# Third chunk's loads in parts, and one piece moved in the order of a mixture-of-experts kernel

## The chip, the cores and the metric

The kernel runs on one core of one Trainium2 chip. The metric is the device time of one execution in microseconds; lower is better. The core's engines are TensorE (PE; its weight loads are listed apart as PEld), VectorE (DVE), ScalarE (ACT), GpSimd (POOL) and SyncE (SP), which issues most of the DMAs. Each engine works through its own instructions in the order in which the program gives them, and waits for others by semaphores.

## The reference

Attention over q, k and v of shape (4, 8, 576, 64) makes x of shape (2304, 512); a mixture of eight experts over x makes the output.

```python
# attention, for each batch and head
q_d, k_d, v_d = means of q, k, v over 4 neighbouring tokens      # 144 of them
out_d = softmax(scale * q_d k_d^T) v_d, repeated 4 times
scores = scale * q k^T, kept where |i - j| < 4                   # a window of 7 tokens
x = out_d + softmax(scores) v                                    # (2304, 512)
# experts
P = exp(x w_gate - max); 8 times: P /= rows' sums; P /= columns' sums; P *= N / E
out = sum over e of P[:, e] * (relu(x w1[e]) w2[e])              # w1 512x1024, w2 1024x512
```

## The kernel before, in words

**Chunks and units of attention.** The 576 groups of four tokens (144 for each batch) are cut into six chunks: three small ones of 64 groups (256 tokens) and three of 128 groups (512 tokens). The third chunk (`c` = 2) covers groups 128 to 191 and so lies on both sides of a batch's end at 144. A small chunk is one load unit for all heads, a large one two, so there are nine units `u` (`lunits`); the third chunk is `u` = 2. For each unit three tiles are loaded: a window of k, q, and a window of v (`l_load_win`, `l_load_q`). `l_parts` says into how many parts such a load falls: eight for the third chunk (four groups of heads by two batches), four for the second chunk and for the two units each of the fourth and fifth, two for those of the last. A k or v part of the third chunk is two DMAs, a q part one.

**The windowed attention** (`l_gen`) is VectorE's: for each unit four products with k (L1162) and their sums (L1188), a softmax, and four products with v (L1238) and their sums (L1311). The down-sampled attention (`d_gen`) is made of small matmuls on PE, with ScalarE between them; its inputs are sums over the loaded tiles that GpSimd makes (`p_gen`, L1415 and L1419) and that go through memory. `x_gen` joins both into the chunk's x, split into a high part xh and a low part xl.

**The experts.** The list `order` holds pairs of a piece and an expert. A piece is one chunk or the first two together; a small chunk alone has two tiles of 128 tokens, (0, 1) and a large chunk have four. Each pair is eight steps, one for each 128 of the 1024 hidden columns; such a step is called a unit of the experts here, and they are counted from 0 along `order`. Each step loads 256 KB of w1 (L1004) and 256 KB of w2 (L1009), splits both into a high part on ScalarE (L2233) and a low part on GpSimd (L2256) or VectorE (L2252), and runs 12 matmuls of the first layer (L2100), the split of the hidden tile (ScalarE L2164, VectorE L2167), and three matmuls for each tile in the second (L2134 to L2136). The weights have six raw buffers, three steps ahead. A step of a two-tile piece takes half of PE's time and the same loads and splits as one of a four-tile piece.

The first three pairs are chunk 0 with experts 0, 1 and 2 (steps 0 to 23); then (0, 1) with 3, 4 and 5 (24 to 47), the third chunk with 3 (48 to 55), (0, 1) with 6, chunk 0 with 7, the third chunk with 4 (72 to 79), chunk 3 with 3 (80 to 87), the third chunk with 5 (88 to 95), and so on. A pair's result is copied out to memory (spilled) while attention is not done. When attention ends, the pairs that are finished by then (`n_done`) stay, the rest of the list is put in a new order, and later stages do most of the remaining work by a Strassen scheme with seven products in place of eight.

**What sets the order of the work.** A planner in the program (`sched`) runs when the kernel is built. It has a clock for each engine, for SyncE's issuing (`clk["sp"]`) and for the transfers (`clk["dma"]`), and generators that each offer their next step with the time at which it can start; the earliest step is emitted, a rank decides between equals. `ld_gen` is the generator for the loads of the units `u` = 2 on: when the products of the unit before have read its k tile (`k_free`) it emits the whole load of k and of q, and when they have read its v tile (`v_free`) that of v. `m_next` is the number of the expert steps whose first layer has been emitted. The function `dma(kb)` advances both clocks and returns the time at which the planner takes the data to be there. All these loads, and the weight loads, are on SyncE's one queue, in the order emitted; a weight load waits there until its raw buffer has been read.

Of the kernel before, what the change touches and what calls it, by code (L numbers as in the profile page):

```python
# [8 lines left out]
F32 = mybir.dt.float32  # L9
# [793 lines left out]
def attention_moe_kernel(  # L803
# [11 lines left out]
    B, H, S, D = q.shape  # L815
# [3 lines left out]
    R = 4  # L819
# [4 lines left out]
    NF = FF // 128  # L824
# [11 lines left out]
    def is_small(c):  # L836
        return chunks[c][1] == 64
# [50 lines left out]
    ap1 = att.enter_context(tc.tile_pool(name="ap1", bufs=1, side="right"))  # L888
# [7 lines left out]
    def mask_of(c):  # L896
        i = edged.index(c)
        return mask[:, i * 2 * R * W:(i + 1) * 2 * R * W]
# [24 lines left out]
    def segs(t0, n):  # L923
        done = 0
        while done < n:
            b, g = divmod(t0 + done, SD)
            step = min(n - done, SD - g)
            yield done, step, b, g
            done += step


    clk = {"pe": 0.0, "dve": 0.0, "act": 0.0, "pool": 0.0, "dma": 0.0, "sp": 0.0, "port": 0.0}
# [25 lines left out]
    def dma(kb, *deps):  # L958
        clk["sp"] = max([clk["sp"]] + list(deps)) + 0.35
        clk["dma"] = max(clk["dma"], clk["sp"] + 0.6) + 0.05 + kb * 0.55  # L960
        return clk["dma"] + 2.0
# [85 lines left out]


    lunits = [(c, hh) for c in range(NC) for hh in range(1 if is_small(c) else 2)]
    l_q, l_k, l_v, l_out = {}, {}, {}, {}  # L1050
    l_done = {}
    x_taken = {}
    lo_keys = []
# [1 line left out]
    def l_parts(c, hh):  # L1055
        t0, n = chunks[c]
        m = n // 2
        return [
            (m * i + off // 2, k_ // 2, b, g // 2, (0 if is_small(c) else 4 * hh) + 2 * i)
            for i in range(128 // m) for off, k_, b, g in segs(t0, n)  # L1060
        ]

    def l_load_q(u, s0=0, sn=2, eng=None):
        if u >= len(lunits):
            return
        c, hh = lunits[u]
        if s0 == 0:
            l_q[u] = (ap1.tile([128, 2, 2 * R, D], F32, tag="lq", name="lq"), [])
        t, ready = l_q[u]
        for p0, m, b, g, h0 in l_parts(c, hh):  # L1070
            (eng or nc.sync).dma_start(
                out=t[p0:p0 + m, s0:s0 + sn].rearrange("p h r d -> p h (r d)"),
                in_=q[b, h0 + s0:h0 + s0 + sn, 2 * R * g:2 * R * (g + m), :].rearrange(
                    "h (p r) d -> p h (r d)", r=2 * R
                ),
            )
        ready += [dma(2 * sn)] * sn

    def l_load_win(u, src, dst, step=2, before=None):
        if u >= len(lunits):  # L1080
            return
        c, hh = lunits[u]
        t = ap2.tile([128, 2, WR, D], F32, tag="lw", name="lw")
        if c == 0:
            nc.gpsimd.memset(t[0:1, 0:step, 0:R - 1, :], 0.0)
        if c == NC - 1:
            nc.gpsimd.memset(t[96:128, :, WR - (R - 1):WR, :], 0.0)

        def win(p0, m, b, g, h0, lo, hi):
            if u + (src is v) and hi - lo > 2 * R:  # L1090
                win(p0, m, b, g, h0, lo, lo + 2 * R)
                return win(p0, m, b, g, h0, lo + 2 * R, hi)
            row = (b * H + h0 + s0) * S + 2 * R * g - (R - 1) + lo
            nc.sync.dma_start(  # L1094
                out=t[p0:p0 + m, s0:s0 + step, lo:hi, :].rearrange("p h r d -> p h (r d)"),
                in_=bass.AP(src.tensor, row * D, [[2 * R * D, m], [S * D, step], [1, (hi - lo) * D]]),
            )

        ready = []
        for s0 in range(0, 2, step):  # L1100
            if before is not None:
                before(s0, step)
            for p0, m, b, g, h0 in l_parts(c, hh):
                if c == 0 and h0 + s0 == 0:
                    win(p0, 1, b, g, h0, R - 1, WR)
                    win(p0 + 1, 15, b, g + 1, h0, 0, WR)
                    win(p0 + 16, m - 16, b, g + 16, h0, 0, WR)
                elif c == NC - 1 and h0 + s0 + step == H and 2 * R * (g + m) == S:
                    win(p0, m - 16, b, g, h0, 0, WR)
                    win(p0 + m - 16, 15, b, g + m - 16, h0, 0, WR)  # L1110
                    win(p0 + m - 1, 1, b, g + m - 1, h0, 0, WR - (R - 1))
                else:
                    win(p0, m, b, g, h0, 0, WR)
            ready += [dma(7 * step / 2)] * step
        dst[u] = (t, ready)

    alone = [True]
# [216 lines left out]
            p2_t[r] = max(clk["act"], t_p2[r]) if r < 2 else t_p2[r]  # L1334

    def ld_gen():
        for u in range(1, len(lunits) - 1):
            while u not in k_free or u >= U1 and ((u, 1) not in s_read or (u, 0) not in s_read):
                yield None
            t = max([k_free[u]] + [s_read[u, s] for s in (0, 1) if u >= U1])  # L1340
            yield t + HOP, "sp", 0.0, False
            l_load_win(u + 1, k, l_k)
            yield t + HOP, "sp", 0.0, False
            l_load_q(u + 1)
            while u not in v_free or u >= U1 and (u, 2) not in s_read:
                yield None
            t = max([v_free[u]] + [s_read[u, 2] for _ in (0,) if u >= U1])
            yield t + HOP, "sp", 0.0, False
            l_load_win(u + 1, v, l_v)


    halves = [(b, hf) for b in range(B) for hf in range(2)]
# [714 lines left out]
    m_next = [0]  # L2067
# [316 lines left out]
    with tc.manual_schedule():  # L2384
# [10 lines left out]
        EH = 3  # L2395
        order = [
            ((0,), 0), ((0,), 1), ((0,), 2), ((0, 1), 3), ((0, 1), 4), ((0, 1), 5), ((2,), 3), ((0, 1), 6), ((0,), 7),
            ((2,), 4), ((3,), 3), ((2,), 5), ((3,), 4), ((2,), 6), ((3,), 5), ((3,), 6), ((3,), 7),
        ]
        last = [((1, 2), 7)]  # L2400
        order += [(p_, e) for e in reversed(range(EH)) for p_ in ((3,), (1, 2))]
        for c, e in order:
            for f in range(NF):
                units.append((e, f, lambda: wa))
                todo.extend(p_todo(len(units) - 1))
        l_load_win(0, k, l_k, step=1, before=lambda h_a, h_n: l_load_q(0, h_a, h_n, None if h_a else nc.scalar))
        d_load()
        l_load_win(0, v, l_v)
# [20 lines left out]
        for big in (True, False):  # L2429
# [7 lines left out]
            for c in edged:  # L2437
                if is_small(c) == big:
                    continue
                t0, n = chunks[c]  # L2440
                at_ = [pb for pb in range(0, n + 1, 2) if (t0 + pb) % SD == 0]
                assert len(at_) == 1
                z = WR * at_[0] // 2
                a, z = z - (R - 1) if at_[0] else z, z + R - 2 if at_[0] < n else z - 1
                dst = mask_of(c)
# [88 lines left out]
        th["lo"] = Thread(lo_gen())  # L2534
        th["raw"] = Thread(raw_gen())
        th["ld"] = Thread(ld_gen())
        for i in range(n_cv[0]):
            w1_done[i], w2_done[i] = w_ready[i]
# [9 lines left out]
        n = m_end[0] // NF * NF  # L2548
# [360 lines left out]
```

## Time and profile before

| | |
|---|---|
| median of 3 runs | 1576.42 us (1576.12 to 1576.99) |
| the profiled execution | 1578.05 us |
| its span, first to last instruction | 1576.3 us |
| granted clock of TensorE, mean share | 0.999 |
| PE busy | 1562.4 us, 99% of the span |
| VectorE, GpSimd, ScalarE busy | 1340.4, 1071.8, 827.1 us |
| tiles spilled (DMA issues of spill<-sp) | 40 |

Times in the trace are microseconds from the span's first instruction. A row of the timeline gives start, duration, engine, line, operation, tile written and tiles read, shape and the number of like instructions merged; in brackets stands the engine's idle time before it and what ended it. "SPq" is SyncE's queue, and its durations are those of issuing. A matmul's record lasts longer than the time after which PE can start the next, so neighbouring records overlap.

### The profile page before, as it was taken

How to read it: one execution, taken by the hardware profiler on the slowest of the kernel's cores; microseconds unless marked ns; L12 is line 12 of the kernel's file. 1: busy time of each engine (PE TensorE's matmuls, PEld its weight loads, DVE VectorE, ACT ScalarE, POOL GpSimd, SP SyncE). 2: the span in 40 equal slices, each digit the busy share in tenths (PEclk: the TensorE clock that was granted, in tenths of full speed). 3: DMA queues.
4: the chain of work that ended last, by engine and by line, in shares of the span. 5: the costliest groups of instructions: out<-in, count | busy, mean ns of one | idle time of the engine just before them, and what ended most of it. 6: DMA issues, size and time to landing. Idle time of an engine off the chain costs nothing.

```text
span 1576.3 us, 24605 instructions
## 1 busy us (share of the span) xinstructions
PE 1562.4 (99%) x8220; PEld 1321.4 (84%) x8220; DVE 1340.4 (85%) x1880; ACT 827.1 (52%) x1763; POOL 1071.8 (68%) x998
## 2 busy tenths in 40 slices
PE   9999999999999999999999999999999999999998
PEld 7788888888888888889999988888888888888887
DVE  8688998778988687478999797999999999999987
ACT  4564554555455534365555545555555555555553
POOL 5698666868685600278777548877877787877872
PEclk9999999999999999999999999999999999999999
DMA  8878676768585645513332372212221222221102
GB/s 197 209 207 209 166 182 156 217 178 231 149 218 135 185 136 174 159 52 102 99 117 73 110 218 82 74 54 67 60 72 57 74 59 75 62 68 54 48 14 54
DMA packets 230701, 191.23 MB, mean 121 GB/s; under 512 B 26478, under 2 KB 188462, under 8 KB 230574
## 3 DMA queue, kind: packets, MB, share of 16 engines
q1 hardware_dynamic: 224046, 178.39, 41.9%
q10 hardware_dynamic: 6528, 11.28, 2.0%
q8 instruction: 64, 1.05, 0.3%
q14 instruction: 63, 0.52, 0.1%
HBM read 167.42 MB, written 22.18 MB: 120 GB/s over the span
## 4 chain that ended last, share of the span: by engine, by line
PE 93%; issue 2%; DVE 2%; DMA 1%; SPq 1%; POOL 1%; ACT 1%; ACTq 0%; POOLq 0%; DVEq 0%
PE psm L588 27%; PE psm L600 19%; PE psh L2100 18%; PE psm L783 7%; PE psy L2134 6%; PE psy L2135 6%; PE psy L2136 6%; PE pss L1725 1%; PE psg L1905 1%; SPq L1094 1%; DMA r<-in_moe_w_dram 0%; PE psx L1849 0%; PE psd L1787 0%; PE psd L1758 0%; DMA dr<-in_v_dram 0%
## 5 line engine op out<-in xcount | busy, mean ns | idle before, releaser
L571 POOL TENSOR_TENSOR o<-r,o 128x512 fp32r<-128x512 f32 x126 | 165.8, 1316 | 87.9 <-ACT o L567 87.4
L2256 POOL TENSOR_TENSOR w1l<-r,w1h 128x512 fp32r<-128x512 f32 x112 | 158.4, 1414 | 81.2 <-ACT w1h L2233 74.5
L2256 POOL TENSOR_TENSOR w2l<-r,w2h 128x512 fp32r<-128x512 f32 x114 | 157.3, 1380 | 28.0 <-ACT w2h L2233 26.9
L588 PE MATMUL psm<-th,o 128*128 128x512 f32 x512 | 173.1, 389 | 0.0
L2134 PE MATMUL psy<-w2h,hh 128*128 128x512 f32 x408 | 165.4, 405 | 0.0
L622 DVE TENSOR_TENSOR acc<-psm,acc 128x512 f32<-128x512 f32 x216 | 144.6, 682 | 21.0 <-PE psm L600 20.8
L2135 PE MATMUL psy<-w2l,hh 128*128 128x512 f32 x408 | 159.5, 391 | 0.0
L2136 PE MATMUL psy<-w2h,hl 128*128 128x512 f32 x408 | 159.4, 391 | 0.0
L600 PE MATMUL psm<-hx,o 128*128 128x512 f32 x564 | 151.1, 389 | 0.0
L2164 ACT ACTIVATE hh<-psh 128x512 fp32r<-128x512 f32 (+1 forms) x136 | 67.6, 497 | 158.4 <-PE psh L2100 149.3
L571 POOL TENSOR_TENSOR o<-xh,o 128x256 fp32r<-128x256 f32 x132 | 111.2, 849 | 50.6 <-ACT o L567 38.4
L2167 DVE SCALAR_TENSOR_TENSOR hl<-psh,hh 128x512 fp32r<-128x512 f32 (+1 forms) x136 | 76.2, 560 | 73.2 <-ACT hh L2164 73.0
L2233 ACT ACTIVATE w2h<-r 128x512 fp32r<-128x512 f32 x133 | 83.7, 629 | 91.3 <-PE psy L2136 25.8
L588 PE MATMUL psm<-xh,o 128*128 128x512 f32 x384 | 131.2, 389 | 0.3 <-DVE hl L2352 0.3
L2100 PE MATMUL psh<-xhs,w1h 128*128 128x256 f32 (+1 forms) x384 | 124.7, 325 | 0.3 <-ACT xhs L1866 0.3
L600 PEld LDWEIGHTS psm<-hx,o 128*128 128x128 f32 x564 | 105.8, 188 | 22.0
L2100 PE MATMUL psh<-xhs,w1l 128*128 128x256 f32 (+1 forms) x384 | 122.5, 319 | 1.5 <-DVE w1l L2252 1.5
L2100 PE MATMUL psh<-xls,w1h 128*128 128x256 f32 (+1 forms) x384 | 122.3, 319 | 0.2
L567 ACT ACTIVATE o<-r 128x512 fp32r<-128x512 f32 x139 | 87.3, 628 | 55.4 <-PE psm L600 35.5
L588 PEld LDWEIGHTS psm<-th,o 128*128 128x128 f32 x512 | 96.1, 188 | 20.1
L1311 DVE TENSOR_REDUCE lo<-prod 128x256 f32<-128x1792 f32 x32 | 109.4, 3420 | 0.4
L571 POOL TENSOR_TENSOR xh<-xh,xh 128x256 fp32r<-128x256 f32 x32 | 24.8, 782 | 118.1 <-ACT xh L567 118.1
(346 smaller groups left out, 4574.4 us busy)
## 6 DMA issues: line engine op xcount, KB each, us to landing
r<-in_moe_w_dram SPq DMA_DIRECT2D x367, 256.0 KB
xh<-in_moe_w_dram SPq DMA_DIRECT2D x108, 128.0 KB
spill<-sp ACTq DMA_DIRECT2D x40, 256.0 KB
s<-spill SPq DMA_DIRECT2D x40, 256.0 KB
xl<-in_moe_w_dram SPq DMA_DIRECT2D x68, 128.0 KB
g<-gd SPq DMA_DIRECT2D x16, 256.0 KB
sums<-dr SPq DMA_DIRECT2D x36, 64.0 KB
r2x<-in_moe_w_dram SPq DMA_DIRECT2D x9, 256.0 KB
```

Of the source, the lines that this page charges most:

```text
L567: self.nc.scalar.activation(out=self.get(v)["h"], in_=self.w_view(l, r, ps), func=AF.Copy)
L571: (self.nc.gpsimd if pool else self.nc.vector).tensor_tensor(out=o["l"], in0=self.w_view(l, r, ps), in1=o["h"].bitcast(F32), op=ALU.subtract)
L588: self.nc.tensor.matmul(out=ps, lhsT=wt[:, k], rhs=xt[:, k], start=start and n == 0, stop=n == 5, skip_group_check=not start,)
L600: self.nc.tensor.matmul(out=ps, lhsT=wt[:, a, 128 * m:128 * m + 128], rhs=ht, start=start and n == 0, stop=n == 5, skip_group_check=not start,
L622: self.nc.vector.tensor_tensor(out=self.get(o[0]), in0=self.get(a[0]), in1=self.get(b[0]), op=op)
L783: self.nc.tensor.matmul(out=ps, lhsT=self.at_tile(ht, t), rhs=wt[:, a], start=start and n + t % 2 == 0, stop=n == 5, skip_group_check=not ...
L1311: nc.vector.tensor_reduce(out=ot[:, :, h % 2], in_=pr.rearrange("p r w d -> p r d w"), axis=AX.X, op=ALU.add,)
L2100: nc.tensor.matmul(out=ps, lhsT=w[:, kk], rhs=x[:, kk], start=(kk == 0 and j == 0), stop=(kk == 3 and j == 2),)
L2134: nc.tensor.matmul(out=ye[z], lhsT=hh[:, ts], rhs=h2, start=(f2 == 0), stop=False)
L2135: nc.tensor.matmul(out=ye[z], lhsT=hh[:, ts], rhs=l2, start=False, stop=False)
L2136: nc.tensor.matmul(out=ye[z], lhsT=hl[:, ts], rhs=h2, start=False, stop=(f2 == NF - 1))
L2256: nc.gpsimd.tensor_tensor(out=l, in0=r, in1=h.bitcast(F32), op=ALU.subtract)
```

## The change

The two load functions become generators, `l_q_parts` and `l_win_parts`, that stop after each part; the old names run them to the end at once. A q load is announced (`l_q[u]`) only when all its parts are out. The planner's clock is charged for each part by itself, with 0.4 us of SyncE more for each part of k and v. In `ld_gen` the loads go through `paced`, which for `u` = 2 alone waits after each part (for v, after the first and then after every second one) until `m_next` has moved, so that another expert step has been emitted; and k of `u` = 2 waits until eight steps have been. In `order`, the third chunk with expert 5 stands before chunk 3 with expert 3.

```diff
-    def l_load_q(u, s0=0, sn=2, eng=None):
+    def l_load_q(*a, **z):
+        for _ in l_q_parts(*a, **z):
+            pass
+
+    def l_load_win(*a, **z):
+        for _ in l_win_parts(*a, **z):
+            pass
+
+    def l_q_parts(u, s0=0, sn=2, eng=None):
...
-        for p0, m, b, g, h0 in l_parts(c, hh):
+        for n, (p0, m, b, g, h0) in enumerate(l_parts(c, hh)):
+            if n:
+                yield
+            t_in = dma(sn / 4)
             (eng or nc.sync).dma_start(
...
-        ready += [dma(2 * sn)] * sn
-
-    def l_load_win(u, src, dst, step=2, before=None):
+        ready += [t_in] * sn
+        l_q[u] = q_tile[u]
+
+    def l_win_parts(u, src, dst, step=2, before=None):
...
-            for p0, m, b, g, h0 in l_parts(c, hh):
+            for n, (p0, m, b, g, h0) in enumerate(l_parts(c, hh)):
+                if n:
+                    yield
+                clk["sp"] += 0.4
+                t_in = dma(7 * step / 16)
...
-            ready += [dma(7 * step / 2)] * step
+            ready += [t_in] * step
...
     def ld_gen():
+        n_alone = 3 * NF
+
+        def paced(u, it, of=1):
+            for i, _ in enumerate(it):
+                n = m_next[0]
+                while u == 2 and i % of == 0 and m_next[0] == n:
+                    yield None
+
         for u in range(1, len(lunits) - 1):
             while u not in k_free or u >= U1 and ((u, 1) not in s_read or (u, 0) not in s_read):
                 yield None
+            while u == 1 and m_next[0] < NF:
+                yield None
             t = max([k_free[u]] + [s_read[u, s] for s in (0, 1) if u >= U1])
             yield t + HOP, "sp", 0.0, False
-            l_load_win(u + 1, k, l_k)
+            yield from paced(u + 1, l_win_parts(u + 1, k, l_k))
             yield t + HOP, "sp", 0.0, False
-            l_load_q(u + 1)
+            yield from paced(u + 1, l_q_parts(u + 1))
             while u not in v_free or u >= U1 and (u, 2) not in s_read:
                 yield None
             t = max([v_free[u]] + [s_read[u, 2] for _ in (0,) if u >= U1])
             yield t + HOP, "sp", 0.0, False
-            l_load_win(u + 1, v, l_v)
+            yield from paced(u + 1, l_win_parts(u + 1, v, l_v), 2)
...
-            ((2,), 4), ((3,), 3), ((2,), 5), ((3,), 4), ((2,), 6), ((3,), 5), ((3,), 6), ((3,), 7),
+            ((2,), 4), ((2,), 5), ((3,), 3), ((3,), 4), ((2,), 6), ((3,), 5), ((3,), 6), ((3,), 7),
```

## Rows read from the trace of the kernel before

**Rows 1.** The page's busy times: engine, us, share of the span, instructions.

```profile
PE 1562.4 (99%) x8220; PEld 1321.4 (84%) x8220; DVE 1340.4 (85%) x1880; ACT 827.1 (52%) x1763; POOL 1071.8 (68%) x998
```

**Rows 2.** PE's waits: line, whom it waited for, us in total, times, longest.

```profile
PE psh L2100 <- DVE w1l L2252: 1.5, 2, 1.2
...
PE pss L1725 <- ACT qz L1675: 1.0, 1, 1.0
...
PE psd L1758 <- ACT pt L1763: 0.4, 1, 0.4
...
PE psx L1849 <- DVE lo L1311: 0.3, 1, 0.3
```

**Rows 3.** SyncE's queue in time, 66 to 117 us: start, us of issuing, what.

```profile
66.32 0.37 SPq L1004 DMA_DIRECT2D r<-in_moe_w_dram  x1
66.74 6.38 SPq L1094 DMA_DIRECT2D lw<-in_k_dram  x16
73.25 0.36 SPq L1009 DMA_DIRECT2D r<-in_moe_w_dram  x1
...
76.85 6.70 SPq L1071 DMA_DIRECT2D lq<-in_q_dram  x8
...
108.89 8.08 SPq L1094 DMA_DIRECT2D lw<-in_v_dram  x16
```

**Rows 4.** ScalarE in time, 78 to 121 us.

```profile
78.24 0.63 ACT L2233 ACTIVATE w2h<-r 128x512 fp32r<-128x512 f32 x1 [4.25 <-DMA r<-in_moe_w_dram]
78.78 0.60 ACT L1675 ACTIVATE qz<-psd 64x160 f32<-64x160 f32 x2
...
120.71 0.64 ACT L2233 ACTIVATE w2h<-r 128x512 fp32r<-128x512 f32 x1 [3.74 <-DMA r<-in_moe_w_dram]
```

**Rows 5.** PE in time, 67 to 263 us.

```profile
67.08 0.39 PE L2100 MATMUL psh<-xhs,w1l 128*128 128x256 f32 x1 [1.25 <-DVE w1l L2252]
...
75.17 1.33 PE L1666 MATMUL psd<-ident,dr 80*64 80x80 f32 x32
...
77.71 0.39 PE L2136 MATMUL psy<-w2h,hl 128*128 128x512 f32 x1
79.11 0.80 PE L1725 MATMUL pss<-kz,qz 128*80 128x144 f32 x4 [1.01 <-ACT qz L1675]
...
114.90 0.28 PE L2100 MATMUL psh<-xhs,w1h 128*128 128x256 f32 x1
...
263.07 0.28 PE L2100 MATMUL psh<-xhs,w1h 128*128 128x256 f32 x1
```

**Rows 6.** Windows: length, busy of PE, PEld, DVE, ACT, POOL, clock, DMA share, GB/s.

```profile
66.00:74.00 8.00, 6.66 (x53) 5.59 (x54) 7.82 (x15) 6.32 (x16) 5.44 (x5) 1.00 0.54 139
...
84.00:108.00 24.00, 23.74 (x169) 21.04 (x168) 20.14 (x18) 15.99 (x40) 22.64 (x21) 1.00 0.78 230
```

**Rows 7.** VectorE in time, 66 to 251 us.

```profile
66.34 0.68 DVE L2252 TENSOR_TENSOR w1l<-r,w1h 128x512 fp32r<-128x512 f32 x1
...
69.12 1.42 DVE L2252 TENSOR_TENSOR w1l<-r,w1h 128x512 fp32r<-128x512 f32 x1
...
114.66 2.01 DVE L1162 TENSOR_TENSOR prod<-lq,lw 128x1792 f32<-128x1792 f32 x1
...
124.04 3.07 DVE L1162 TENSOR_TENSOR prod<-lq,lw 128x1792 f32<-128x1792 f32 x1
...
146.66 2.01 DVE L1238 TENSOR_TENSOR prod<-lw,psd 128x1792 f32<-128x1792 f32 x1
...
250.89 0.68 DVE L1887 TENSOR_TENSOR xls<-psx,xhs 128x512 fp32r<-128x512 f32 x1
```

**Rows 8.** Windows around the moved piece, columns as in rows 6.

```profile
335.00:389.00 54.00, 54.00 (x357) 47.52 (x357) 37.12 (x52) 36.44 (x85) 43.29 (x37) 1.00 0.80 215
389.00:411.00 22.00, 22.00 (x102) 18.21 (x101) 21.90 (x12) 8.73 (x15) 16.18 (x17) 1.00 0.70 196
...
436.00:460.00 24.00, 24.00 (x154) 21.74 (x153) 18.56 (x24) 14.49 (x30) 18.27 (x16) 1.00 0.87 223
```

More of the change, by code (lines that the diff above doesn't have):

```diff
@@ L1049, in attention_moe_kernel @@
     lunits = [(c, hh) for c in range(NC) for hh in range(1 if is_small(c) else 2)]
-    l_q, l_k, l_v, l_out = {}, {}, {}, {}
+    l_q, l_k, l_v, l_out, q_tile = {}, {}, {}, {}, {}
     l_done = {}
@@ L1067, in l_load_q @@
         if s0 == 0:
-            l_q[u] = (ap1.tile([128, 2, 2 * R, D], F32, tag="lq", name="lq"), [])
-        t, ready = l_q[u]
-        for p0, m, b, g, h0 in l_parts(c, hh):
+            q_tile[u] = (ap1.tile([128, 2, 2 * R, D], F32, tag="lq", name="lq"), [])
+        t, ready = q_tile[u]
+        for n, (p0, m, b, g, h0) in enumerate(l_parts(c, hh)):
+            if n:
+                yield
+            t_in = dma(sn / 4)
             (eng or nc.sync).dma_start(
```

## The prediction, made before the changed kernel was run

> **What bounds the kernel now.** I read the page's busy shares first: TensorE (PE) is busy 1562.4 of 1576.3 us [rows 1], so all its idle time is 13.9 us, and nothing that leaves its work alone can win more. Next I asked PE's waits for the stretch in which the third chunk's loads go out. Four waits stand there: 1.5 us for the low parts of w1, 1.0 us for qz, 0.4 us for pt and 0.3 us for lo [rows 2], together 3.2 us. The reader is to see that these are all that the loads can have cost PE. Then the SyncE queue and ScalarE's timeline, to see which of the four the loads cause.
>
> **The wait that the loads cause.** The eight k parts are 16 DMAs; SyncE issues them in one run from 66.74 for 6.38 us, 0.40 us each, between the w1 load at 66.32 and the w2 load of the same unit at 73.25 [rows 3]. That w2 load is what ScalarE waits for: it idles 4.25 us until 78.24 and only then does qz, the next in its order, at 78.78 [rows 4]. PE had delivered qz's source from 75.17 on and reaches the scores that need qz after the matmul at 77.71, which ends at 78.10; it starts them at 79.11, having idled 1.01 us [rows 5]. That is the 1.0 us of rows 2.
>
> **The change part by part.**
>
> k parts. The first leaves where the run began, in unit 8 (the 67.08 row lies in it [rows 5]; m_next is then 9), the others one a unit up to m_next 16. The 16 DMAs stay 16, at 0.40 us: 0.8 us of SyncE a unit. A unit is about 2.96 us long, from unit 22 at 114.90 to unit 48 at 263.07 [rows 5]: 148.2 us for two short units and 24 of double length, 50 short ones in all. Its two weight loads cost about 0.4 us each (0.37 and 0.36 [rows 3]), so SyncE is asked for 1.6 us in 2.96. The w2 load can then go out near 66.8 and, with the 4.99 us it took from issue to use, serve ScalarE at 71.8. ScalarE was free for it at 78.24 less 4.25, 73.99, so w2h is no longer late; qz then waits only for PE, whose 32 small matmuls from 75.17 last 1.33 us to 76.50. With 0.60 us for its two pieces [rows 4], qz is done near 77.2, before PE wants it at 78.10. The 1.01 us go. Late next would be a w1l, which waits for VectorE (below).
>
> q parts. Eight DMAs ran from 76.85 for 6.70 us [rows 3]. The one PE wait of rows 2 that lies behind their first issue is the 1.01 already counted, and the w2 load of 73.25 causes it, so 0. They now take m_next 16 to 23.
>
> v parts. Sixteen DMAs ran from 108.89 for 8.08 us [rows 3]; ScalarE idled 3.74 us for the weights behind them [rows 4], PE did not at all: the buffered weights cover it. So 0 there, too. The new places are m_next 23 to 27, two parts to most units.
>
> What comes later. The third chunk's first product on VectorE needs all of q. Its last part leaves after unit 22's first layer or a unit later, 116.3 to 119.3, and lands 3 to 5 us on (4.99 is the row I have): the product moves from 114.66 to between 119 and 124. But the second product ran only at 124.04 [rows 7], because the reduce between them sat behind the late weights. So 5 to 10 us at the first product are 1 to 5 us at the second. v's last part leaves in unit 27, 114.90 + 2 x 2.96 + 3 x 5.93 = 138.6, lands by 143.6, and is wanted at 146.66 [rows 7]. PE needs the chunk's x at 263.07 [rows 5]; VectorE finished it at 250.89 + 0.68 = 251.57 [rows 7]. Margin 11.5 us against 1 to 5: cost 0.
>
> The moved piece. The eight units of (2,) with expert 5 now precede the first four-tile piece of chunk 3. PE was 100% busy in the stretches on both sides, 335 to 389, 389 to 411 and 436 to 460 [rows 8]: there is no idle time to win. PE's work is the same matmuls. The set finished by the end of attention, the first 14 pairs, does not depend on the swap inside it, so spills and the Strassen stages are the same. What it can cost is in 389 to 411, where 24 two-tile units now run without a break: bounds 0 and +5.0 (last rival). I take 0, since 335 to 389 held the same mix for 16 units at 43.29 of 54 us of GpSimd and no PE idle.
>
> The planner's clock. The list of instructions is made by a planner with a clock of its own. It now charges every k or v load 0.4 us more of SyncE for each part, and its transfer time goes by parts: a load in eight parts keeps its 7 units, one in four has 3.5, one in two 1.75. So the order of later work can shift anywhere up to the end of attention. No row shows what other order follows. Nearest are PE's short waits of rows 2: I bound it by losing one more of the longest (+1.25) and by losing none of the other three (-2.2), and take 0.
>
> **The sum.** 1578.05 us (span 1576.3 and 1.75 around it) less 1.0 is 1577.0 for an execution like the profiled one. The median of the runs lies 1.63 us under it, so I forecast 1576.42 - 1.0 = 1575.4 us.
>
> The trace bears on one rule here. During the k run the DMA engines were 0.54 busy at 139 GB/s, though 0.78 at 230 GB/s just after [rows 6]: the engines had room while SyncE issued. The Trainium skill, "DMA: Bandwidth & Descriptors", section "Issuing engines are not separate DMA queues", says that DMAs share 16 engines whoever issues them, and that the sequencer's time to initiate them "is usually small relative to the DMA itself". By that, the weights wait for transfers, not for issues, and spreading them leaves the time at 1576.4; by the row 6.38 us of issuing is what was late.
>
> **Rivals.**
>
> No gain (1576.4): another short wait takes the 1.0. For it: ScalarE does its work in order, PE met four such waits in 40 us, and a part of k or q now stands before nearly every weight load from unit 8 to 23, so each lands 0.4 to 0.8 us later than it could. Against: three loads of weights lie ahead in buffers, over 8 us.
>
> All four gone (1573.2): 1576.4 less the 3.2 of rows 2. For it: the waits for w1l come with VectorE busy on products, 1.42 us for a low part at 69.12 and 0.68 at 66.34 [rows 7], and weights arriving on time would let GpSimd take them. Against: 67.08 lies only 0.34 after the first k DMA, so its 1.25 us cannot come from them; only the new charges could move it.
>
> Slower (1580.4): low parts of weights come late in 389 to 411. Four long units ran there, with 16.18 us of GpSimd [rows 8]; eight short ones need eight low parts more, at 1.17 us (43.29 us over 37 instructions in 335 to 389 [rows 8]): 25.5 us in about 23.7 (eight units of 2.96). VectorE was 21.90 of 22 busy there [rows 8], so a low part that it takes over waits in its order. If four of the eight units meet a wait like 67.08's 1.25, 5.0 us are lost, less 1.0: +4.0. It decides from one such wait on, and is slower by over 0.2% from four. Against it: 84 to 108 had two-tile units and VectorE 20.14 of 24 busy, GpSimd 22.64 of 24, and PE idled only 0.26 [rows 6]; and 436 to 460 ran these same eight units with GpSimd at 18.27 of 24 [rows 8], the rest on VectorE. The Trainium skill, "SBUF — State Buffer", section "SBUF: two separate sides", says VectorE and GpSimd hold the port they share exclusively, for a whole instruction; the 1.42 against 0.68 agrees, and it makes this rival's low parts dearer.
>
> **Chances.** Forecast 0.45, no gain 0.25, all four gone 0.17, slower 0.13. I predict 1575.4 us; the range 1572.4 to 1578.6 holds the first three, each with a wait or two like the 1.25 more or less, and leaves out most of the slower case. 0.2% is 3.2 us, about what a measurement tells from no change. Faster by more: 0.19 (the third case and a tail of the first); slower by more: 0.12; within: 0.69.
>
> **What would show it.** Right: no run of 16 issues on SyncE after 66, the w2 load following its w1 by under 1.5 us, ScalarE without a 4 us gap at 74, PE without the wait for qz; VectorE's first product of the third chunk near 119 to 124 and x still before unit 48; PE 100% busy from 389 to 460. Wrong: a PE wait of over 1 us between 70 and 125 for another weight, low parts that PE waits for in 389 to 411, or an end of attention that leaves other than 40 spilled tiles.

## The result: 11 us slower, and the profile after

The changed kernel takes 1587.7 us (median of four runs, 1583.66 to 1587.99), the kernel before 1576.7 us: a ratio of 1.0064, with a 95% interval of 1.0047 to 1.0082. The forecast was 1575.4 us, with a range of 1572.4 to 1578.6. The profiled execution of the changed kernel took 1583.66 us, with a span of 1581.9: 5.6 us above the span before.

The page's busy times, in the columns of rows 1:

```profile
PE 1564.5 (99%) x8220; PEld 1321.6 (84%) x8220; DVE 1349.8 (85%) x1882; ACT 826.4 (52%) x1763; POOL 1066.9 (67%) x996
```

PE has the same number of matmuls and is busy 2.1 us longer; the rest of the 5.6 us is idle time.

**Where the loads go out, it went as forecast.** SyncE's queue, which answers to [rows 3]:

```profile
68.63 0.37 SPq L1004 DMA_DIRECT2D r<-in_moe_w_dram  x1
69.08 0.72 SPq L1106 DMA_DIRECT2D lw<-in_k_dram  x2
69.90 0.36 SPq L1009 DMA_DIRECT2D r<-in_moe_w_dram  x1
73.36 0.39 SPq L1004 DMA_DIRECT2D r<-in_moe_w_dram  x1
73.80 0.88 SPq L1106 DMA_DIRECT2D lw<-in_k_dram  x2
```

The run of 16 is gone: two DMAs of k stand between weight loads. PE's waits between 50 and 125 us, against the four of [rows 2] (line, whom it waited for, total, times, longest):

```profile
PE psd L1813 <- ACT pt L1789: 1.0, 1, 1.0
PE psd L1784 <- ACT pt L1789: 0.5, 1, 0.5
PE psx L1875 <- DVE lo L1327: 0.4, 1, 0.4
PE psy L2160 <- ACT sp L2231: 0.3, 1, 0.3
```

The waits for qz and for w1l are gone; a wait of 1.0 for pt has come. No wait is over 1.0 us. (Line numbers are those of each kernel, so the same instruction has another one here.)

**The time was lost at the end of attention,** called the handover below. VectorE's timeline of the changed kernel (start, duration, instruction, and in brackets the idle time before it and what ended it):

```profile
548.86 0.30 DVE L1965 TENSOR_REDUCE stmp<-lg 128x1 f32<-128x144 f32 x1
549.22 0.48 DVE L2824 MEMSET acc<- 128x512 f32 x1
552.31 1.57 DVE L2824 MEMSET acc<- 128x512 f32 x3 [2.61 <-DMA spill<-sp]
553.79 0.63 DVE L2684 TENSOR_TENSOR bsum<-xh,xl 128x512 f32<-128x512 f32 x1
...
554.93 0.27 DVE L1973 TENSOR_REDUCE stmp<-psd 1x1 f32<-1x128 f32 x1
```

And the same place in the kernel before:

```profile
551.54 0.30 DVE L1939 TENSOR_REDUCE stmp<-lg 128x1 f32<-128x144 f32 x1
551.76 0.68 DVE L2167 SCALAR_TENSOR_TENSOR hl<-psh,hh 128x512 fp32r<-128x512 f32 x1
552.97 0.28 DVE L1947 TENSOR_REDUCE stmp<-psd 1x1 f32<-1x128 f32 x1 [0.53 <-PE psd L1944]
553.30 2.11 DVE L2798 MEMSET acc<- 128x512 f32 x4
```

When attention ends, the planner begins a new phase by zeroing four sums (`acc`), and the softmax over the gates needs two reduces. Before, the second reduce (into `stmp`) stands ahead of the four MEMSETs; after, it stands behind them and two more instructions. And the last three MEMSETs wait 2.61 us for the DMA that reads a spill out: the new sums take memory that spill buffers had. PE needs the reduce:

```profile
551.25 0.40 PE L2126 MATMUL psh<-xh,w1l 128*128 128x512 f32 x1
555.26 0.38 PE L1979 MATMUL psd<-stmp,ones 1*128 1x1 f32 x2 [3.62 <-DVE stmp L1973]
555.57 0.54 PE L2126 MATMUL psh<-xh,w1h 128*128 128x512 f32 x1
555.91 0.63 PE L2126 MATMUL psh<-xl,w1h 128*128 128x512 f32 x1
556.33 0.63 PE L2126 MATMUL psh<-xh,w1l 128*128 128x512 f32 x1
...
558.89 0.58 PE L2162 MATMUL psy<-w2h,hl 128*128 128x512 f32 x1
559.31 0.39 PE L2160 MATMUL psy<-w2h,hh 128*128 128x512 f32 x1
```

It idles 3.62 us, and then its matmuls start 0.43 us apart until 559.31, where 0.23 is usual. The windows of that stretch and of one of [rows 8], with their columns (length, busy of PE, PEld, DVE, ACT, POOL, granted clock, DMA share, GB/s):

```profile
389.00:411.00 22.00, 21.38 (x142) 18.25 (x141) 18.91 (x18) 12.35 (x24) 19.28 (x17) 1.00 0.97 252
555.90:559.30 3.40, 3.40 (x9) 2.67 (x8) 3.10 (x9) 1.34 (x3) 0.00 (x0) 0.50 0.68 222
559.40:562.80 3.40, 3.40 (x18) 2.80 (x17) 2.43 (x7) 0.63 (x1) 0.00 (x0) 1.00 0.21 79
```

In the second row the granted clock is 0.50 (1.2 GHz) for the 3.4 us behind the wait, then 1.00 (2.4 GHz) again: 9 records in place of 18, so 1.7 us lost. With the idle time that is 5.3 us.

**An account by stretches.** Waits alone miss matmuls that run slowly, so I use one more measure, worked out from PE's records: for each matmul the time to the next one's start, less the median of that time for its line and shape, summed where positive ("lost" below, us). It depends somewhat on how the matmuls are grouped: with another grouping by shape the stretches move by up to 1.3 us and before's 26.8 becomes 29.7, while the differences in the last column but one move by no more than 0.4. The first 50 us differ between executions (PE's 411th matmul starts at 48.9 to 55.8 us, though PE's list is the same there in all of them), so the sum from 50 us on is compared. "Time" is the median of all runs less that of the kernel before in the same session.

| kernel | 50–100 | 100–150 | 150–350 | 350–550 | 550–600 | from 50 on, less before's 26.8 | time |
|---|---|---|---|---|---|---|---|
| before | 7.6 | 0.5 | 5.3 | 5.3 | 3.2 | 0 | 0 |
| changed | 5.6 | 1.7 | 5.7 | 8.0 | 7.3 | +6.2 | +11.0 |
| changed, run again (e4) | 5.7 | 1.6 | 6.0 | 8.5 | 8.2 | +8.1 | +9.6 |
| e1, moved piece only | 7.9 | 0.5 | 5.3 | 6.0 | 2.8 | +0.4 | +0.3 |
| e2, all but moved piece | 6.1 | 1.8 | 7.8 | 28.9 | 2.3 | +25.1 | +27.6 |
| e3, zeroing later | 5.6 | 1.7 | 6.5 | 8.6 | 2.0 | +2.3 | +4.1 |
| e5, charges of before | 7.0 | 0.7 | 9.3 | 9.1 | 3.3 | +7.4 | +4.7 |
| e6, charges only | 6.6 | 2.2 | 6.7 | 7.8 | 3.1 | +4.4 | +5.5 |
| e7, charges and moved piece | 6.3 | 1.8 | 6.8 | 8.8 | 8.6 | +10.3 | +10.8 |
| e8, pacing only | 6.8 | 0.9 | 6.2 | 11.2 | 3.0 | +7.7 | +7.2 |
| f1, old list, spread | 11.1 | 9.6 | 4.8 | 6.0 | 3.2 | +12.6 | +12.2 |
| g1, old list, spread by twos | 10.2 | 5.4 | 5.0 | 5.5 | 3.3 | +7.2 | +7.5 |
| g2, old list, k alone by twos | 8.5 | 0.6 | 5.3 | 6.3 | 3.2 | +2.1 | +3.4 |
| g4, new list, no spread | 9.7 | 1.9 | 5.7 | 7.8 | 7.5 | +10.6 | +12.7 |
| g5, old list, k behind one w2 | 6.8 | 0.6 | 5.3 | 5.5 | 2.9 | −0.7 | +0.4 |

In the changed kernel the stretch of the loads gains 2.0 us, and 8 us are lost: 1.2 in 100 to 150, 2.7 in 350 to 550, 4.1 at the end of attention. The profiled execution is the fastest of its four; run again, the profiled one had the clock at half for 6.83 us behind the same wait (3.7), where this one has 3.41. The other three of the first four have no profile.

### The profile page after: what moved, and what is told of

Its sections match the earlier page's. It is cut to its first block, busy times and chain, and to the rows that moved or that the text cites. A ratio compares the mean times of both kernels' runs of the same rounds, so it can differ in the third digit from the quotient of the medians.

```text
span 1581.9 us, 24580 instructions
## 1 busy us (share of the span) xinstructions
PE 1564.5 (99%) x8220; PEld 1321.6 (84%) x8220; DVE 1349.8 (85%) x1882; ACT 826.4 (52%) x1763; POOL 1066.9 (67%) x996
## 4 chain that ended last, share of the span: by engine, by line
PE 88%; DVE 4%; DMA 3%; issue 1%; SPq 1%; POOL 1%; ACT 1%; ACTq 0%; POOLq 0%; DVEq 0%
PE psm L588 26%; PE psm L600 19%; PE psh L2126 16%; PE psm L783 7%; PE psy L2160 5%; PE psy L2162 5%; PE psy L2161 5%; DMA r<-in_moe_w_dram 2%; PE psh L2366 1%; PE pss L1751 1%; SPq L1106 1%; SPq L1423 1%; DVE prod L1254 1%; PE psg L1931 0%; DVE acc L794 0%
## 5 line engine op out<-in xcount | busy, mean ns | idle before, releaser
L2282 POOL TENSOR_TENSOR w1l<-r,w1h 128x512 fp32r<-128x512 f32 x111 | 153.5, 1383 | 78.8 <-ACT w1h L2259 73.3
```

Source lines behind the costliest of these rows:

```text
L2282: nc.gpsimd.tensor_tensor(out=l, in0=r, in1=h.bitcast(F32), op=ALU.subtract)
```

## The experiments

Two words are kept apart below. The list is the order of instructions on PE, VectorE, ScalarE and GpSimd, which the planner makes; the spread is where the pieces of k, q and v stand among SyncE's issues. The change makes a new list and a spread at once.

### Which edit costs it? (e1, e2, e3, e4)

e1 is the kernel before with the moved piece alone, the last line of the change.

> The kernel before with the moved piece alone (loads in one run as before). Theory A (the loss is made where attention hands over: VectorE's zeroing of four sums waits for a spill and PE waits for VectorE): here the list has the reduce that PE waits for ahead of the zeroing, so no wait of over 1 us for stmp and no fall of the clock there; time within 3 us of before, 1574 to 1579. Rival B (three two-tile pieces in a row starve PE of low parts): PE waits for low parts or hl in 389 to 411 add 3 us or more, 1580 or above.

1577.08 us, ratio 1.0000 (0.9991 to 1.0009). The moved piece alone costs nothing, as forecast, and its rival (low parts late in 389 to 411) falls.

e2 is the changed kernel with that line taken back.

> The changed kernel with the old order of pieces. Its list has the zeroing (two tiles, not four) ahead of the reduce that PE waits for, as in the changed kernel. Theory A: if the spill has not landed, PE waits 2 to 4 us for stmp near 550 and the clock falls, 1579 to 1588; if the spill is earlier here, no wait and about 1575. Rival B: no loss at 389 to 411 and a time of 1575 to 1577, whatever the list has at the handover. Both: the wait for qz near 78 is gone and the first 100 us are about 1 us shorter.

1604.39 us, ratio 1.0183 (1.0154 to 1.0211). PE's waits from 385 to 420 us, and one window of them:

```profile
PE psd L1813 <- DMA dv<-sums: 6.9, 1, 6.9
PE psd L1717 <- DMA dq<-sums: 5.5, 1, 5.5
PE psx L1875 <- DVE xl L1913: 3.7, 1, 3.7
```

```profile
391.00:414.50 23.50, 10.37 (x41) 6.62 (x42) 16.93 (x12) 2.47 (x6) 5.34 (x7) 0.50 0.51 114
```

The x of the fourth chunk is late. In the old order PE needs it at unit 80, near 389 us. VectorE finished it at 375.05 + 0.68 = 375.7 in the kernel before, at 408.8 in the changed one:

```profile
408.13 0.68 DVE L1913 TENSOR_TENSOR xl<-psx,xh 128x512 fp32r<-128x512 f32 x1
```

So the moved piece puts eight units that need only old data in front of it, and is worth some 18 us (1604.39 against the 1586.39 of the changed kernel in the same session, e4 below) to a list that has the fourth chunk late. The lateness grows from chunk to chunk: 3.7 us for the third chunk's x (251.57 before, 254.59 + 0.69 = 255.28 after), 33 us for the fourth's.

e3 is the changed kernel with the four sums zeroed later, once the gates are ready:

```diff
+        to_zero = []
...
-                nc.vector.memset(acc[z], 0.0)
+                to_zero.append(acc[z])
...
                 scale_early()
+                for z in to_zero:
+                    nc.vector.memset(z, 0.0)
```

> The changed kernel, with the four sums zeroed only after the gates are ready, some 40 us later, so that no instruction of VectorE waits for a spill before the reduce. Theory A: PE's wait of 3.6 us for stmp and the half clock after it go, 1576 to 1579 (what is left over before is the 1 to 3 us of waits at 404 and 508). Rival B: the time stays above 1582, since what is lost is lost before 510.

1580.92 us, ratio 1.0023 (1.0014 to 1.0032). The three longest waits of its PE between 50 and 600 us:

```profile
PE psg L1931 <- DVE xl L1913: 1.0, 1, 1.0
PE psd L1813 <- ACT pt L1789: 1.0, 1, 1.0
PE psy L2162 <- DVE hl L2193: 0.6, 1, 0.6
```

No wait for stmp is left. The time lies between the two theories: 5.5 us under the changed kernel of the same session (e4 below), 6.8 under its first four runs, and still 4.1 above the kernel before. e4 is the changed kernel once more, beside these:

> The changed kernel once more, for a second profile and more times: its four executions so far are 1583.7 and 1587.4 to 1588.0. Theory A: the executions differ in when the spill lands and in how long PE's clock stays at half speed after the wait, so a profile of a longer one shows a wait of over 3.6 us for stmp or more than 3.4 us of half clock, 4 us together. Rival B: the longer ones lose it before 510 us.

1586.39 us, ratio 1.0062 (1.0047 to 1.0077); a wait of 3.7 for stmp.

### Charges or spread? (e5 to e8)

The first theory was that the new charges of the planner's clock spoil its list and the spread is harmless. e5 is the changed kernel with the charges of before:

```diff
-            t_in = dma(sn / 4)
...
-        ready += [t_in] * sn
+        ready += [dma(2 * sn)] * sn
...
-                clk["sp"] += 0.4
-                t_in = dma(7 * step / 16)
...
-            ready += [t_in] * step
+            ready += [dma(7 * step / 2)] * step
```

> The changed kernel with the planner's clock charged as before (a k or v load 7 units once, a q load 4, no 0.4 us for each part); parts, pacing and the moved piece stay. In its list the reduce that PE waits for stands ahead of the zeroing again, and the fourth chunk's x is done 9 units earlier. Theory A (the new charges spoil the order of the later work; spreading the loads is harmless): 1575 to 1577.5, no PE wait of over 0.6 us after 100, none for qz near 78. Rival B (the spreading itself makes attention late): 1579 or above, with waits of PE for VectorE in 400 to 560 as in the changed kernel.

1581.89 us, ratio 1.0030 (1.002 to 1.004). The handover's wait is gone and so is that for qz, but there are new ones: 1.6 for hl at 356, 1.5 for dq at 274, 0.6 for sp at 372.

e6 has the new charges, but no pacing and the old order of pieces; e7 has the moved piece besides:

```diff
-                while u == 2 and i % of == 0 and m_next[0] == n:
+                while False and i % of == 0 and m_next[0] == n:
```

> The new charges alone: loads in one run, old order of pieces. Theory A: slower, 1579 or above, since the fourth chunk's x is planned at unit 80, where PE needs it, and data come later than the planner takes them to. Rival B: 1576 to 1577.5, like before.

> The new charges and the moved piece, loads in one run. Its list has the zeroing ahead of the reduce, as in the changed kernel. Theory A: the handover's wait of 2 to 4 us for stmp and the fall of the clock come without any spreading of loads: 1580 to 1588. Rival B: no such wait, 1576 to 1578.

e6: 1582.76 us, ratio 1.0041 (1.0025 to 1.0057). e7: 1587.99 us, ratio 1.0065 (1.005 to 1.008), with the handover's wait back:

```profile
PE psd L1979 <- DVE stmp L1973: 3.9, 1, 3.9
```

So the charges (5.5 us by themselves) and the moved piece (nothing by itself) make up the whole loss, 10.8 us, without any spread. (Both keep the wait of k for eight expert steps and the later announcing of q.) e8 has the pacing alone, with the charges and the order of before:

> The spreading of the third chunk's loads alone: old charges, old order of pieces. Theory A: 1575 to 1577.5; the wait for qz near 78 is gone, and the fourth chunk's x comes in unit 79, in time for unit 80. Rival B: PE waits for the sums in memory and for x in 385 to 410, as in the run with the parts and the old order (6.9, 3.7 and 5.5 us), 1585 or above.

1584.37 us, ratio 1.0045 (1.003 to 1.006): no wait for qz, but three for hl of 2.5 in all, 1.6 of it at 354, and 11.2 us lost in 350 to 550. Neither theory holds as put: each of the four, which all make the planner choose again, loses 4.7 to 10.8 us, e5, e6 and e8 in other places than the changed kernel.

### Is it the order at the handover? (f2, f4)

f2 is the kernel before, whose second reduce is held until the phase has ended, so that the MEMSETs come ahead of it:

```diff
         yield t + HOP, "dve", 0.3, False
+        while m_stop[0] is None:
+            yield None
         nc.vector.tensor_reduce(out=rs[0:1, 1:2], in_=ps, axis=AX.X, op=ALU.max)
```

> The kernel before, with one edit: the softmax over the gates holds its second reduce until the planner's first phase has ended, so that VectorE zeroes the four sums ahead of it (places 458 to 461 of its list, the reduce at 463, before: the reduce ahead). Loads, charges and order of parts stay. Theory 'the order of zeroing and reduce decides the handover': TensorE waits for that reduce at 554 us, about 1.5 us (554.25 wanted, 552.4 + 2.11 + 0.6 + 0.28 ready) or more where the zeroing waits for the spills too; the time is 1578 to 1584, by whether TensorE's clock falls behind it. Rival 'the wait at the handover only shows other lateness': 1576 to 1577.3, no wait over 0.5 us there.

1577.59 us, ratio 0.9999 (0.9990 to 1.0009). VectorE and PE there:

```profile
553.18 2.11 DVE L2800 MEMSET acc<- 128x512 f32 x4
...
555.75 0.27 DVE L1949 TENSOR_REDUCE stmp<-psd 1x1 f32<-1x128 f32 x1
```

```profile
556.07 0.38 PE L1955 MATMUL psd<-stmp,ones 1*128 1x1 f32 x2 [1.06 <-DVE stmp L1949]
```

The theory fails on the size: the order alone makes PE wait 1.06 us, the clock does not fall, and no time is lost that can be measured. What the changed kernel has besides is the 2.61 us for the spill, which left at 546.9 to 547.3, about 2 us ahead of the first MEMSET; in f2 the spills left 8 and 6 us ahead of it. So I read the 3.62 us as the order and the spill's wait together, with the clock behind them; the spill's wait alone was not tried.

f4 is the kernel before with e3's edit:

> The kernel before, with the four sums zeroed only once the gates are ready (the edit that gave the changed kernel 6.8 us back). Theory 'that edit takes away the handover's wait and nothing else': the kernel before has no such wait, so 1576 to 1577.5. Rival 'the later zeroing is a gain by itself, and the changed kernel was not better for the handover': 1569 to 1573.

1576.92 us, ratio 0.9997 (0.9988 to 1.0006). By itself the later zeroing gains nothing, so what e3 gave back was the handover's.

### Is any other list worse? (f3, g3)

```diff
-        begin = {"pe": 36.6, "dve": 38.2, "act": 39.0, "pool": 42.3, "port": 38.2, "sp": 42.0, "dma": 48.0}
+        begin = {"pe": 36.6, "dve": 38.2, "act": 39.0, "pool": 42.3, "port": 38.2, "sp": 42.0, "dma": 48.4}
```

> The kernel before with the planner's clock of transfers started 0.4 us later (48.4 in place of 48.0 us): no load, tile or instruction is added, but the lists of TensorE (495 lines of difference) and VectorE (135) come out otherwise from about unit 11 on; the reduce stays ahead of the zeroing and the chunks keep their places but for two units. Theory 'any list but this one loses a few short waits': 1579 to 1584, over waits of 0.5 to 2 us in several places. Rival 'only lists that the late parts push back lose': 1576 to 1577.5.

> The kernel before with the planner's clock of transfers started 0.4 us earlier (47.6 in place of 48.0), the other way than in f3: again no load, tile or instruction is added, and TensorE's list differs from that of before in 400 lines, VectorE's in 174. Theory 'the list of before is a lucky one among near ones, and any other loses some us': 1579 to 1584. Rival 'near lists go to both sides, f3 was a chance': 1574 to 1577.5.

f3 (48.4): 1580.31 us, ratio 1.0019 (1.001 to 1.0028). g3 (47.6): 1579.85 us, ratio 1.0016 (1.0007 to 1.0025). One constant of the planner, moved by 0.4 us either way, costs 2.7 to 2.8 us; nothing else of the kernel is changed. g3's longest waits of PE that the kernel before does not have:

```profile
PE psd L1920 <- ACT gs L1912: 1.3, 1, 1.3
PE psy L2134 <- ACT hh L2164: 1.3, 1, 1.3
PE psd L1758 <- ACT pt L1763: 1.0, 1, 1.0
```

Two nudges are few, but both lose, and so does every other list here that differs from that of before from unit 6 to 12 on (the changed kernel's, e2, e3, e5 to e8). e1's differs only from unit 80 on, f2's from the handover on, and they lose nothing.

### List and spread apart (f1, g4)

f1 keeps the list of before to the last instruction and only puts off the issue of the third chunk's pieces, one behind each weight load:

```diff
+        if pend:                      # in raw_next, behind the weight's dma_start
+            pend.pop(0)[1]()
...
+    def put_part(u, what, fn):
+        if u == 2:
+            pend.append((what, fn))
+        else:
+            fn()
```

What is still pending goes out ahead of its first reader.

> The kernel before with its planner, its charges and its order of parts untouched, so that TensorE, VectorE and ScalarE keep their lists to the last instruction; only the issue of the third chunk's k, q and v pieces is put off, one piece behind each raw weight load, on the same queues. Theory 'the re-made plan costs the time, the spreading does not': the wait for qz at 79 us (1.01) shrinks to under 0.3, the gap of 4.25 us on ScalarE goes, no new wait of TensorE over 0.5 us comes, and the time is 1575.4 to 1577.0, ratio 0.999 to 1.000. Rival 'pieces that arrive late cost it whatever the list': the first product of the third chunk waits on VectorE, its list is held up behind it, and the time is 1579 or more.

1589.73 us, ratio 1.0076 (1.0064 to 1.0089): worse than the changed kernel. GpSimd's timeline:

```profile
83.05 1.41 POOL L1436 TENSOR_TENSOR dr<-lw 128x256 f32<-128x256 f32 x2 [8.64 <-DMA lw<-in_k_dram]
...
133.09 1.40 POOL L1436 TENSOR_TENSOR dr<-lw 128x256 f32<-128x256 f32 x2 [8.05 <-DMA lw<-in_v_dram]
```

GpSimd makes the sums of k and v for the down-sampled attention, and low parts of weights. In the old list its sums come at 76.5 us, and with the pieces late it waits there 8.64 us, with low parts of weights behind it. PE then waits twice for w1l from GpSimd, 9.1 us in all, and the clock falls behind both (3.41 us at 87.6, 6.83 at 135.4).

g4 is the mirror: the list of the changed kernel to the last instruction, with k, q and v out in one run each at the place of the first part.

```diff
+                if u == 2 and n == 0:
+                    for at in l_parts(c, hh):
+                        win(*at, 0, WR)
...
+                if u == 2:
+                    continue
```

> The mirror of f1: TensorE, VectorE, ScalarE and GpSimd have the list of the changed kernel to the last instruction (86 lines of it differ in nothing but line numbers), but the third chunk's k, q and v go out in one run each, where the first part stood. Theory 'the new list costs the time, not the pieces': the handover wait near 555 us stays and the time is 1585 to 1589. Rival 'the pieces cost it': under 1580, with the third chunk's first product back at 115 us and the fourth chunk's x near 375.

1589.85 us, ratio 1.0082 (1.0069 to 1.0096). PE's waits between 50 and 600 us:

```profile
PE psd L1991 <- DVE stmp L1985: 3.8, 1, 3.8
PE psd L1704 <- ACT od L1834: 2.8, 1, 2.8
PE psg L1943 <- DVE xl L1925: 1.0, 1, 1.0
```

So the new list loses 12.7 us without the spread. Its runs do not leave when those of the kernel before did: they stand at the new list's places, k at 71.27, q at 99.70 and v at 123.38 us, where the kernel before has 66.74, 76.85 and 108.89 [rows 3]. e7 bears on whether it is this lateness: it has no spread either, its runs leave at 71.04, 81.51 and 108.99, the handover's wait is the same, and it loses 10.8. Within the new list the spread looks like a help: in g4 a wait of 2.8 for od appears at 83 us, with the clock at half behind it, and 50 to 100 us loses 9.7 in place of 5.6. The medians do not prove it: 1.0064 against 1.0082, with intervals that overlap.

### Can the spread gain its 1.0 us? (g1, g2, g5, g6)

g1 is f1 with two parts behind each weight load, g2 the same for k alone.

> As f1 (the list of the kernel before on TensorE, VectorE, ScalarE and GpSimd, the third chunk's pieces put between the weight loads), but two parts behind each weight load in place of one, so that k is out within four weight loads of its start, as is v, and no piece is later than 5 us behind where it was. Theory 'f1 lost its 12 us because GpSimd's list came to the sums of pieces that were not there': GpSimd waits under 1.5 us for k and for v (8.6 and 8.0 in f1), TensorE not over 1 us for w1l from GpSimd, the wait for qz is gone, and the time is 1575.0 to 1577.0. Rival 'pieces between the weight loads cost by themselves': 1579 or more, with waits for weights all along 68 to 125 us.

> As g1, but k alone is put between the weight loads, two parts behind each; q and v go out in one run as before. By the prediction's reading the k run makes the whole wait for qz (1.01) and q and v cost nothing: 1575.0 to 1576.6, the same as g1 within 0.5. Rival 'the wait for qz stands for another one that takes its place': 1576.5 to 1577.5, with the sum of TensorE's waits between 60 and 125 us unchanged near 3 us.

g1: 1584.69 us, ratio 1.0051 (1.0038 to 1.0064). g2: 1580.59 us, ratio 1.0018 (1.001 to 1.0027). I had expected both to be free. In g2, qz is ready in time and w2h is made at 74.68 in place of 78.24, as the prediction had it; but k is out at 78.3 in place of 73.1. Its first DMA leaves 1.5 us later (the w1 load ahead of it is 0.8 later in this execution), the three weight loads between its pieces take SyncE 2.4 us, of which one takes 1.60, and its own DMAs wait 1.6 us for earlier DMAs to land. That one weight load, then GpSimd, and one of PE's waits:

```profile
75.19 1.60 SPq L1004 DMA_DIRECT2D r<-in_moe_w_dram  x1
```

```profile
81.65 1.43 POOL L1437 TENSOR_TENSOR dr<-lw 128x256 f32<-128x256 f32 x2 [6.96 <-DMA r<-in_moe_w_dram]
```

```profile
PE psh L2122 <- POOL w1l L2278: 2.0, 1, 2.0
```

The row of GpSimd names a weight load as what ended its wait, but the instruction reads k alone. Idle time has moved from ScalarE (4.25 us, [rows 4]) to GpSimd, which idled 2.63 us at this place in the kernel before, and PE pays 2.0 for it in place of 1.0. g1 has besides a wait for v's pieces, in a window of 60 to 150 us:

```profile
POOL dr L1437 <- DMA lw<-in_v_dram: 7.4, 1, 7.4
```

PE waits 4.6 us for w1l from GpSimd there, in two waits.

g5 keeps the k run whole and puts one load of w2 ahead of it; g6 adds e3's edit.

```diff
+        while pend:                   # k alone, all behind the next weight load
+            pend.pop(0)[1]()
```

> The kernel before, lists of TensorE, VectorE, ScalarE and GpSimd untouched, with one edit to SyncE's: the load of w2 that stood behind the third chunk's 16 k DMAs stands ahead of them, and the run of 16 stays whole. Theory 'g2 lost because k was out 5 us later (78.3 in place of 73.1) and GpSimd waited 7 us for it': k is out near 74.5, GpSimd's sums start at 76.5 to 78.5 in place of 81.65, TensorE waits for no w1l near 83 and not for qz (under 0.3): 1575.3 to 1576.8, about 1 us under the kernel before. Rival 'every piece that is later than in the kernel before costs TensorE more than the wait for qz': 1578 or more.

> g5, and the four sums zeroed only once the gates are ready (as in f4, which was 0.3 us under the kernel before, within its interval). Theory: both savings are real and add: 1574.8 to 1576.4. Rival 'neither can be told from nothing': 1576.5 to 1577.8, as the kernel before.

g5: 1577.42 us, ratio 1.0000 (0.9991 to 1.0009). ScalarE, and PE's waits between 50 and 125 us:

```profile
73.42 0.62 ACT L2254 ACTIVATE w2h<-r 128x512 fp32r<-128x512 f32 x1
76.46 0.62 ACT L1696 ACTIVATE qz<-psd 64x160 f32<-64x160 f32 x2 [2.42 <-DVE psd L1241]
```

```profile
PE psh L2121 <- DVE w1l L2273: 1.5, 2, 1.2
PE psx L1870 <- DVE lo L1330: 0.5, 1, 0.5
PE psd L1779 <- ACT pt L1784: 0.4, 1, 0.4
```

The wait for qz is gone, nothing has come but 0.2 for lo, and 0.7 us less is lost from 50 us on; the median does not show it. One reason may be that the kernel before does not pay the 1.0 in every execution. e1, f2 and f4 have its list and its loads up to here, so that their profiles are more samples of the same stretch: the wait for qz is 1.3 us in f2, not listed in f4, and in e1

```profile
PE pss L1725 <- ACT qz L1675: 0.3, 1, 0.3
```

In e1 and f4 the clock had fallen to 1.2 GHz for 3.41 us (from 66.8 and 67.2 us), behind the wait for w1l. From the matmul that ends that wait to the scores, the four take 11.9 to 12.3 us; g5 and g6, in which the clock did not fall, take 10.9. So the edit does spare the microsecond where the clock stays up. Where it falls, the kernel before has little or no wait to spare. How often it falls in executions without a profile is not known.

g6: 1576.86 us, ratio 0.9998 (0.9989 to 1.0007). No version that beats the kernel before by a measurable amount was found; e1, f4, g5 and g6 equal it.

## Why the prediction was wrong

**The step that failed is "the planner's clock".** The prediction said that the order could shift anywhere up to the end of attention, and then bounded the cost by +1.25 and −2.2 from the four waits of [rows 2], all between 64 and 97 us, and took 0. The runs put the term at +10.8 us (e7: new charges and moved piece, no spread) to +12.7 (g4: the changed kernel's list, no spread), in place of 0. From 5.5 to 6.8 us of the loss are the handover near 555 us (e3), some 450 us behind the waits that the bound was taken from; the rest is small waits in 100 to 150 and 350 to 550. The list of new charges was also short: a q load is charged by parts as well, so that one in four parts takes 2 units in place of 4. The kernel before had almost no idle time left (13.9 us, [rows 1]), which the prediction read as little to win. I read it now as a list that fits the data's arrival closely, so that another has more to lose than to gain; f3 and g3 agree, but two nudges do not prove it.

**"What comes later" was right for the chunk that it followed and stopped there.** The third chunk's first product came at 120.86 (forecast 119 to 124), its x at 255.28, ahead of unit 48 at 261.50; PE did not wait. The fourth chunk's x, 33 us late, was not looked at.

**"k parts" held.** No run of 16, no gap of 4 us on ScalarE, no wait for qz, and g5 shows that the w2 load behind the run was the cause: with that load issued ahead of the run of 16, w2h was made at 73.42 in place of 78.24 [rows 4]. The Trainium skill, "DMA: Bandwidth & Descriptors", section "Issuing engines are not separate DMA queues", says that the time to initiate a DMA is usually small beside the DMA itself. For one DMA that holds here, 0.40 us of issuing against 4.99 from issue to use of a weight load [rows 3, rows 4]; sixteen in a row held the load behind them up by 6.38. The gain was 0.7 us in g5's profile in place of 1.0, and the medians do not show it. The 1.0 was read from one execution, and other profiles of the same list have 1.3, 0.3 or none.

**"q parts" and "v parts" at 0 do not hold with the list of before.** There they cost 4.1 us (g1 against g2), through GpSimd's sums, which the prediction did not follow: it asked when VectorE and PE need the tiles, not GpSimd. In the new list no run tries them apart. (Its reading that one PE wait lies behind q's first issue left out the 0.3 for lo, at 97.06 us.)

**"The moved piece" at 0 was right (e1), and its rival wrong:** in 389 to 411 PE was busy 21.38 of 22 us, with one wait of 0.6, for hl. What the text missed is what the piece does together with the late fourth chunk (e2): the units that it puts first cover for the chunk.

**The signs named came out nearly all right,** 40 spills among them, and the time was wrong all the same. (Two did not hold throughout: w2 follows its w1 by 1.7 to 2.3 us in several units from 75 us on, and PE has the 0.6 us wait in 389 to 411.) They watched 66 to 125 and 389 to 460 us, and 4.1 us more than before were lost at 555.

**What stays open.** Why the planner's phase ends ahead of the reduce in the new list is not shown; that it does was read from the lists. Which of the new charges re-makes the list, the 0.4 us for each part or the transfer times by parts, was not tried apart. The 4.1 us that e3 leaves were not undone one by one: its profile has several waits of up to 1.0 us, and 2.3 us more lost from 50 us on than before. And the median lies 4 us above the profiled execution; 6.83 us at half clock in place of 3.41, as in e4, would explain 1.7 of them.

## What to carry to other kernels

Where a planner makes the order, an edit of its charges or of one load is an edit of the whole order: cost it by the places where the order is tightest (the ends of phases, where buffers change hands), not by the stretch that the edit is about, and try the new order with the old loads, and the old order with the new loads, apart. When a load is moved later, follow it to every engine that reads the tile: the one that waits may be one whose other work the critical engine needs. Here, with the busiest engine at 99%, a removed wait gave back nothing that the medians show, and every list made anew from an early unit on lost.

## What was not expected of the hardware

The clock falls behind an idle time of PE by different amounts. After 3.62 us of idle time (changed kernel) it was 1.2 GHz for 3.41 us, after 3.7 (e4) for 6.83 us, and through the three waits of e2 for 23.89 us. It fell for 3.41 us at 81.0 in g3, among waits of 1.3 and 0.7, but not behind 1.06 in f2; behind the same wait for w1l at 65 to 67 us (1.2) it fell in f4 and e1 and not in the kernel before or f2. And the first 50 us vary between profiled executions with the same list of PE there: its 411th matmul starts at 48.9 (g3) to 55.8 us (e6), and within 2.3 us of the earliest in all but e6. Two profiles are better compared from the point where the edit begins.
